# Low parts of the weights on GpSimd in block 0, and all kernel blocks of the convolution made in block 0

## The chip, the cores and the metric

The kernel runs on one core of one Trainium2 chip. Its time is the device time of one execution in microseconds; of the kernel before there are three runs, and their median is the time that counts. A profile is one further execution, recorded by the hardware, with a time of its own.

## The reference, cut to what is computed

A layer in two halves on `x` of shape 1 x 2048 x 576, all in float32: a state-space convolution along the sequence, and a feed-forward part of width 4608.

```
mod = (silu(c) @ w_mod).reshape(1, 6, 1, 576)          # sa, ca, ga, sb, cb, gb
h = layernorm(x) * (1 + ca) + sa
P = exp((A * dt)[:, :, None] * arange(2048))           # 576 x 128 x 2048, complex
K = 2 * einsum("dn,dnl->dl", C * dt, P).real           # one kernel of 2048 taps per channel
x = x + ga * (causal_convolution(h, K) + h * D_skip)   # by FFT of length 4096
h = layernorm(x) * (1 + cb) + sb
x = x + gb * (relu(h @ w1) @ w2)                       # w1 576 x 4608, w2 4608 x 576
```

## The kernel before, in words

**Four blocks of the sequence.** The 2048 positions are cut into 4 blocks of 512 (`NB`). For each block there is a convolution, `conv(s)` for s = 0 to 3, and then a feed-forward part over 36 tiles of 128 hidden units (`NF`). The feed-forward part of all four blocks is one loop of 144 tiles in `ffn` (L1401). `conv(0)` and everything that leads to it run ahead of that loop. `conv(1)`, `conv(2)` and `conv(3)` run inside it, one block ahead: `conv(1)` beside tiles 0 to 35, and so on. What runs beside the tiles of a block is a Python generator: `block0`, `block1`, `block2` (L774 to L793).

**The tiles.** float32 precision comes from three products: a weight `r` is rounded to a high part `w` by ScalarE (`hi1`, `hi2`), and the low part is what is left, `r - w` (`lo1`, `lo2`). In block 0 the low parts are computed, three subtractions a tile: 128x640 (L1296), 128x64 (L1307) and 128x512 (L1308). They are also stored to device memory, and blocks 1 to 3 load them from there. `first(g)` makes 14 matmuls of 128x512 into `hps`. ScalarE then makes the high part `hh` of the activation, and VectorE the low part `hl` (L1332). `second(g)` makes 14 more matmuls into the five accumulators `acc`, one tile later. Two buffers hold the raw `r1`, three the raw `r2`, and three each the split `w1` and `w2`; a raw buffer is free when its low part has been computed.

**The convolution kernels.** The 2048 taps fall into four kernel blocks of 512. Kernel block 0 is made ahead of the loop. Kernel blocks 1 to 3 are made by `rest` from tables `W1d`, `Zd`, `W2d` in device memory, for twelve groups of 48 channels (`NH`). For a group, `rots` turns a table of 128 x 2 x 48 x 16 by a complex factor, once for every kernel block. One such turn, `rot`, is four VectorE instructions: two products of 128x1536 (L481, L483) and two sums of 128x768 (L485, L487). Then `products` makes 192 small matmuls into `kps`, in two halves that ScalarE empties into `ke`. The tables come in by DMAs from GpSimd's queue in written order (`load0`, `load2`), ahead of use, into 3 buffers for `W0` and `Z` and 2 for `W2`.

In the kernel before, `block0` makes kernel blocks 1 to 3 of groups 0 to 5 and kernel block 1 alone of groups 6 to 11: 24 turns. `conv(1)` needs no more than that. `block1` loads the tables of groups 6 to 11 once more and makes their kernel blocks 2 and 3: 12 turns.

**What sets the order.** `step(g)` is called four times in a tile and takes work from the block's generator (L1362). The generator yields estimated VectorE microseconds, or `None` for work of TensorE. `rate` gives the work per step that is aimed at; `room` limits what may be taken within any four steps. What a block's generator has not yielded by its last tile is drained there (L1428). In the program that results, a scheduler of the framework decides each engine's order, except for instructions marked as kept in program order. Every engine then runs its own queue in order, and waits at an instruction whose inputs or buffers aren't ready.

Of the kernel before, what the change touches and what calls it, by code (L numbers as in the profile page):

```python
# [10 lines left out]
F32 = mybir.dt.float32  # L11
# [7 lines left out]
P = 128  # L19
# [5 lines left out]
NF = F // P  # L25
G = 96
NG = 6
H = 48
# [21 lines left out]
class KGen:  # L50
# [400 lines left out]
                out=self.k.kd[s][p][64 * t : 64 * t + 64], in_=ke[t::2]  # L451
            )

    def rest(self, psum, plan):

        nc, k = self.nc, self.k
        v = nc.vector.tensor_tensor
        hs = list(plan)
        with ExitStack() as ctx:
            pt = k.pool(ctx, f"kr{len(hs)}", side="right")  # L460
            d = Kept(k.tc, nc.gpsimd).dma_start

            def load0(h):
# [23 lines left out]
                v(out[:, 1], out[:, 1], T[:, 0], op=ALU.add)  # L487
                yield 0.95

            def rots(h, W1, W0, Z):  # L490
                blocks = plan[h]
                a = [W1[:, :, :, 16 * i : 16 * i + 16] for i in range(len(blocks))]
                if blocks[0] == 1:
                    yield from rot(a[0], W0, Z, 0)
                    if len(blocks) > 1:
                        yield from rot(a[1], W0, Z, 1)
                        yield from rot(a[2], a[0], Z, 1)
                else:
                    yield from rot(a[0], W0, Z, 1)
                    yield from rot(a[1], a[0], Z, 0)  # L500

            ke = {}

            def products(h, W1, W2):
                blocks = plan[h]
                na = 16 * len(blocks)
                if h % 6 == 0:
                    ke[h // 6] = pt.tile([P, na, 72], F32, tag=f"ke{na}", bufs=1, name=f"ker_{h}")
                for half in range(2):
                    ps = psum.tile([P, 6, na], F32, tag="cps", bufs=1, name="kps")  # L510
                    for q in range(6):
                        for dd in range(4):
                            ch = dd * 12 + 6 * half + q
                            for r in range(2):
                                nc.tensor.matmul(  # L515
                                    ps[32 * dd : 32 * dd + 32, q, :],
                                    W2[:, r, ch],
                                    W1[:, r, ch],
                                    start=(r == 0),
                                    stop=(r == 1),  # L520
                                )
# [3 lines left out]
                    nc.scalar.activation(  # L525
                        ke[h // 6][:, :, q0 : q0 + 6], ps.rearrange("p q a -> p a q"), AF.Copy
                    )
                    yield None
                if h % 6 == 5:
                    yield -1  # L530
                    for i, s in enumerate(blocks):
# [5 lines left out]
            nxt = [load0(hs[0])]  # L537
            W2 = load2(hs[0])
            nxt.append(load0(hs[1]))
            for _ in range(1 if len(hs) == NH else 7):  # L540
                yield -1
            prev = iter(())
            for i, h in enumerate(hs):
                W0, Z = nxt.pop(0)
                if i + 2 < len(hs):
                    nxt.append(load0(hs[i + 2]))
                na = 16 * len(plan[h])
                bufs = 1 if len(plan[h]) != len(plan[hs[i - 1]]) else 2
                W1 = pt.tile([P, 2, H, na], F32, tag=f"W1{na}", bufs=bufs, name=f"W1r_{h}")
                yield from spread(rots(h, W1, W0, Z), prev, len(plan[h]))  # L550
                prev = products(h, W1, W2)
                if i + 1 < len(hs):
                    W2 = load2(hs[i + 1])
            yield from prev


# [9 lines left out]
class Body:  # L566
# [195 lines left out]
    def main(self, ctx, kg, hooks):  # L762
# [496 lines left out]
    def ffn(self, gens):  # L1259
# [102 lines left out]
        def step(g):  # L1362
# [194 lines left out]
```

## Time and profile before

| what | value |
|---|---|
| median of 3 runs | 1340.26 us (1336.31 to 1343.84) |
| the profiled execution: its time, its span | 1346.28 us, 1344.5 us |
| mean granted TensorE clock | 0.934 |
| first low part `hl` of the activation: tile 0, 36, 72, 108 | 233.6, 570.0, 847.0, 1105.0 us |
| last `hl` (tile 143) | 1328.1 us |
| VectorE, whole span | 895.8 us busy, 1324 instructions |
| GpSimd, whole span | 162.5 us busy, 260 instructions |

The work ahead of the loop takes the first 227 us or so. After it the blocks can be told apart in the trace by the first `hl` of each: block 0 runs to about 562 us, block 1 to about 846, block 2 to about 1106, block 3 to the end. How to read it: in a span of four stages with different limits, the shares over the whole span say little, and each block is looked at by itself. A busy TensorE is not the same as a TensorE at its peak, since the granted clock changes.

### The profile page before, as it was taken

What the parts mean: (1) busy time and instruction counts of PE and PEld (TensorE: products, weight loads), DVE (VectorE), ACT (ScalarE), POOL (GpSimd) and SP (SyncE); (2) the same over time, 40 slices, a digit from 0 to 9 for tenths busy, and PEclk for the clock granted to TensorE, in tenths of its full rate; (3) what the DMA queues carried; (4) which work ended last, traced back from release to release, by engine and by line L of the source; (5) the groups of instructions that cost most, each with busy time, mean ns of one, the idle gap of its engine ahead of it and who ended that gap; (6) DMA issues with size and microseconds to landing.
All of it is one profiled execution on the core that took longest, in us unless ns stands there. A gap on an engine that the chain in (4) does not pass through costs nothing.

```text
span 1344.5 us, 26011 instructions
## 1 busy us (share of the span) xinstructions
PE 1218.3 (91%) x10720; PEld 963.8 (72%) x10720; DVE 895.8 (67%) x1324; ACT 494.6 (37%) x863; POOL 162.5 (12%) x260
## 2 busy tenths in 40 slices
PE   4565686889989998999999999999999999999997
PEld 3344564667768676777777887887888888888885
DVE  5999978997995999768658995467996221111112
ACT  5688523222223422622234225433323352323331
POOL 0656501001100100011001000100000000000000
PEclk9556767999999998999999999999999999999998
DMA  8567972987878877698889995867996667666661
GB/s 269 218 231 291 307 272 80 346 298 273 320 279 288 297 247 290 206 400 322 281 276 339 346 357 160 275 219 271 349 392 189 176 178 230 193 197 199 199 177 53
DMA packets 122379, 345.85 MB, mean 257 GB/s; under 512 B 23916, under 2 KB 24212, under 8 KB 111508
## 3 DMA queue, kind: packets, MB, share of 16 engines
q1 hardware_dynamic: 105364, 226.96, 50.9%
q0 software_dynamic: 16384, 115.85, 23.0%
q8 instruction: 84, 1.38, 0.4%
q10 hardware_dynamic: 512, 1.38, 0.3%
q14 instruction: 35, 0.29, 0.1%
HBM read 262.73 MB, written 81.40 MB: 256 GB/s over the span
## 4 chain that ended last, share of the span: by engine, by line
PE 72%; DVE 14%; DMA 7%; issue 4%; ACT 2%; POOL 1%; ACTq 0%; POOLq 0%; DVEq 0%; SPq 0%
PE acc L1352 29%; PE hps L1326 28%; DMA r<-in_w_dram 4%; PE ps_f L846 4%; PE kps L71 2%; PE ph L71 2%; PE kps L515 2%; PE ps_i L1053 2%; DVE W1r L483 2%; DVE T L481 2%; DMA L2d<-w 1%; DVE W1r L487 1%; DVE W1r L485 1%; DVE T L62 1%; DVE w L1296 1%
## 5 line engine op out<-in xcount | busy, mean ns | idle before, releaser
L1326 PE MATMUL hps<-xh,w 128*128 128x512 f32 x1152 | 393.6, 402 | 1.9 <-issue 1.1
L1352 PE MATMUL acc<-w,hh 128*128 128x512 f32 x1152 | 370.6, 403 | 12.9 <-ACT hh L1331 12.9
L1332 DVE SCALAR_TENSOR_TENSOR hl<-hps,hh 128x512 fp32r<-128x512 f32 x144 | 99.1, 688 | 310.1 <-ACT hh L1331 309.3
L1352 PEld LDWEIGHTS acc<-w,hh 128*128 128x128 f32 x1152 | 216.3, 189 | 60.7 <-ACT hh L1331 14.5
L1326 PEld LDWEIGHTS hps<-xh,w 128*128 128x128 f32 x1152 | 218.5, 190 | 50.2 <-issue 1.6
L1326 PE MATMUL hps<-xl,w 128*128 128x512 f32 x576 | 229.7, 400 | 0.1
L1352 PE MATMUL acc<-w,hl 128*128 128x512 f32 x576 | 223.0, 399 | 0.9 <-DVE hl L1332 0.9
L1331 ACT ACTIVATE hh<-hps 128x512 fp32r<-128x512 f32 x144 | 85.8, 596 | 289.7 <-PE hps L1326 289.4
L1301 ACT ACTIVATE w<-r 128x576 fp32r<-128x576 f32 x141 | 96.7, 686 | 231.0 <-PE acc L1352 219.5
L1291 ACT ACTIVATE w<-r 128x640 fp32r<-128x640 f32 x140 | 102.7, 733 | 92.8 <-DMA r<-in_w_dram 92.8
L1326 PEld LDWEIGHTS hps<-xl,w 128*128 128x128 f32 x576 | 109.3, 190 | 23.9 <-DVE xl L47 0.6
L1352 PEld LDWEIGHTS acc<-w,hl 128*128 128x128 f32 x576 | 107.9, 189 | 24.7 <-DVE hl L1332 2.1
L1326 PE MATMUL hps<-xs,w 128*128 128x512 f32 x288 | 98.6, 413 | 0.0
L71 PE MATMUL kps<-W,W 128*32 128x16 f32 x2304 | 39.9, 211 | 45.3 <-POOL W L68 28.1
L1032 DVE TENSOR_TENSOR Y<-Y,T 128x1152 f32<-128x1152 f32 x60 | 79.4, 1351 | 0.0
L71 PEld LDWEIGHTS kps<-W,W 128*32 128x32 f32 x2304 | 35.1, 144 | 59.0 <-POOL W L68 30.8
L847 ACT ACTIVATE Z<-ps_f 128x288 f32<-128x288 f32 x120 | 48.8, 408 | 70.2 <-PE ps_f L846 68.8
L515 PEld LDWEIGHTS kps<-W1r,W2r 128*32 128x32 f32 x3456 | 44.7, 113 | 37.7 <-issue 19.0
L515 PE MATMUL kps<-W1r,W2r 128*32 128x48 f32 (+2 forms) x3456 | 52.1, 201 | 14.6 <-ACT ker L525 9.3
L1471 POOL DMA_DIRECT2D out_dram<-x x16 | 8.7, 544 | 468.6 <-DVE x L1463 466.3
L1326 PEld LDWEIGHTS hps<-xs,w 128*128 128x128 f32 x288 | 54.0, 191 | 11.3
L1352 PE MATMUL acc<-hl,w 128*128 128x512 f32 x144 | 56.7, 394 | 0.0
(235 smaller groups left out, 1586.6 us busy)
## 6 DMA issues: line engine op xcount, KB each, us to landing
r<-in_w_dram SPq DMA_DIRECT2D x144, 320.0 KB, 7.3
r<-in_w_dram SPq DMA_DIRECT2D x144, 288.0 KB, 5.1
w<-L1d SPq DMA_DIRECT2D x108, 320.0 KB, 3.2
w<-L2d SPq DMA_DIRECT2D x108, 288.0 KB, 2.8
W2r<-W2d POOLq DMA_DIRECT2D x18, 1536.0 KB, 9.2
W2d<-W SPq DMA_DIRECT2D x12, 1536.0 KB, 8.6
Ua<-Ud POOLq DMA_DIRECT2D x15, 1152.0 KB, 9.6
W<-W1d POOLq DMA_DIRECT2D x18, 768.0 KB, 10.6
```

The lines of the kernel that those rows point to most:

```text
L71: self.tc.keep_in_program_order(self.nc.tensor.matmul(*args, **kw))
L481: v(T, X, zi, op=ALU.mult)
L515: nc.tensor.matmul(ps[32 * dd : 32 * dd + 32, q, :], W2[:, r, ch], W1[:, r, ch], start=(r == 0), stop=(r == 1),)
L846: nc.tensor.matmul(o, fc[:, n2, c, :], src(n2), start=True, stop=True)
L847: ev = nc.scalar.activation(Z[:, n2, c], ps[:, :PC], AF.Copy)
L1032: v(y, y, T, op=op or ALU.add)
L1291: copy(g - 1)(w1[g][:, 0], r1[g], AF.Copy)
L1301: copy(g)(w[:, 0:D], r2[g], AF.Copy)
L1326: nc.tensor.matmul(ps, a, x, start=(i == 0), stop=(i == 13))
L1331: nc.scalar.activation(hh, ps, AF.Relu)
L1332: nc.vector.scalar_tensor_tensor(hl, ps, 0.0, hh, op0=ALU.max, op1=ALU.subtract)
L1352: nc.tensor.matmul(acc[i], a, x, start=(f == 0 and seen[i] == 1), stop=(f == NF - 1 and seen[i] == (3 if i < 4 else 2)),)
```

## The change

Three things are changed together.

1. `vec(g)`, the engine that subtracts for the low parts, becomes GpSimd for tiles 3 to 35. For tiles 0 to 2 it stays VectorE. The results and the stores are the same.
2. `rest` makes kernel blocks 1 to 3 of all twelve groups in one pass, in `block0`, in the order 0 to 11: 36 turns. The call in `block1` is gone, and with it the second loads of six groups' tables and the six groups' second pass of small matmuls. The small matmuls of groups 6 to 11 in block 0 are 48 columns wide and not 16.
3. The numbers that set the pace: `room` in block 0 goes from 7.5 to 10.2, `rate` from 2.15 to 2.5 in block 0 and from 1.8 to 1.27 in block 1.

```diff
-    def rest(self, psum, plan):
+    def rest(self, psum):
...
-            def rots(h, W1, W0, Z):
-                blocks = plan[h]
-                a = [W1[:, :, :, 16 * i : 16 * i + 16] for i in range(len(blocks))]
-                if blocks[0] == 1:
-                    yield from rot(a[0], W0, Z, 0)
-                    if len(blocks) > 1:
-                        yield from rot(a[1], W0, Z, 1)
-                        yield from rot(a[2], a[0], Z, 1)
-                else:
-                    yield from rot(a[0], W0, Z, 1)
-                    yield from rot(a[1], a[0], Z, 0)
+            def rots(W1, W0, Z):
+                a = [W1[:, :, :, 16 * i : 16 * i + 16] for i in range(3)]
+                yield from rot(a[0], W0, Z, 0)
+                yield from rot(a[1], W0, Z, 1)
+                yield from rot(a[2], a[0], Z, 1)
...
-            for _ in range(1 if len(hs) == NH else 7):
-                yield -1
+            yield -1
...
         def block0():
             self.x2p.append(self.pool(ctx, "x2b"))
-            yield from kg.rest(
-                self.cps, {h: (1, 2, 3) if h < 6 else (1,) for h in (0, 6, 1, 7, 2, 8, 3, 9, 4, 10, 5, 11)}
-            )
+            yield from kg.rest(self.cps)
...
             yield -1
             self.cvs.close()
-            yield from kg.rest(self.cps, {h: (2, 3) for h in range(6, NH)})
             pool(2)
             yield from self.conv(2)
...
         def vec(g):
-            return (Kept(self.tc, nc.vector) if g < 3 else nc.vector).tensor_tensor
+            return (Kept(self.tc, nc.vector) if g < 3 else nc.gpsimd).tensor_tensor
...
-            room = (7.5, 7.0, 7.0, 7.0)[g // NF] - sum(recent[-3:])
+            room = (10.2, 7.0, 7.0, 7.0)[g // NF] - sum(recent[-3:])
...
-        return (2.15, 1.8, 1.4, 0.5)[b]
+        return (2.5, 1.27, 1.4, 0.5)[b]
```

In the changed kernel the line numbers behind the first of these edits are smaller by up to 14: L1282, L1293, L1294 there are L1296, L1307, L1308 here, L1318 is L1332, and L1016 and L1018 are L1030 and L1032.

**GpSimd's queue in block 0.** Before it holds only DMA issues there. `W2r`, `W` and `Zr` are the tables of one group, each read from its place in device memory.

```order
L47 DMA W2r_3074<-W2d_71 128x3072
L47 DMA W_7_3076<-W1d_84 128x1536
L47 DMA Zr_3077<-Zd_96 128x192
L47 DMA W2r_3233<-W2d_66 128x3072
L47 DMA W_2_3235<-W1d_79 128x1536
L47 DMA Zr_3236<-Zd_91 128x192
```

In the changed kernel the same place, from the load of the fourth group's `W2r` on, reads as follows. `w` is a split weight and `r` its raw form; the two low parts of 64 and 512 columns belong to tiles 5 and 6, those of 640 columns to tiles 7 and 8.

```order
L47 DMA W2r_3268<-W2d_67 128x3072
L47 DMA W_4_3270<-W1d_81 128x1536
L1293 TENSOR_TENSOR w_3339<-r_3071,w_3339 128x64
L1294 TENSOR_TENSOR w_3339<-r_3071,w_3339 128x512
L1293 TENSOR_TENSOR w_3442<-r_3176,w_3442 128x64
L1294 TENSOR_TENSOR w_3442<-r_3176,w_3442 128x512
L1282 TENSOR_TENSOR w_3345<-r_3286,w_3345 128x640
L47 DMA Zr_3271<-Zd_93 128x192
L1282 TENSOR_TENSOR w_3448<-r_3416,w_3448 128x640
L47 DMA W2r_3475<-W2d_68 128x3072
```

The subtractions of two tiles now stand between the loads of one group and those of the next, behind DMAs that wait for a buffer.

**VectorE in block 0, between one `hl` and the next but one.** Before, the turns of the tables (`T`, `W1r`) stand among the subtractions for the low parts (`w<-r,w`).

```order
L1332 SCALAR_TENSOR_TENSOR hl<-hps,hh 128x512
L485 TENSOR_TENSOR W1r_2993<-W1r_2993,T 128x48x16
L487 TENSOR_TENSOR W1r_2993<-W1r_2993,T 128x48x16
L1307 TENSOR_TENSOR w_3094<-r_2942,w_3094 128x64
L481 TENSOR_TENSOR T<-W_6_2967,Zr_2968 128x1536
L1308 TENSOR_TENSOR w_3094<-r_2942,w_3094 128x512
L1296 TENSOR_TENSOR w_3033<-r_3001,w_3033 128x640
L483 TENSOR_TENSOR W1r_3080<-W_6_2967,Zr_2968 128x1536
L483 TENSOR_TENSOR W1r_3239<-W_1_2989,Zr_2990 128x96x16
L485 TENSOR_TENSOR W1r_3080<-W1r_3080,T 128x768
L487 TENSOR_TENSOR W1r_3080<-W1r_3080,T 128x768
L1332 SCALAR_TENSOR_TENSOR hl<-hps,hh 128x512
```

In the changed kernel there are only turns between them.

```order
L1318 SCALAR_TENSOR_TENSOR hl<-hps,hh 128x512
L485 TENSOR_TENSOR W1r_3274<-W1r_3274,T 128x48x16
L487 TENSOR_TENSOR W1r_3274<-W1r_3274,T 128x48x16
L483 TENSOR_TENSOR W1r_3481<-W_3_3062,Zr_3063 128x96x16
L481 TENSOR_TENSOR T<-W_2_2989,Zr_2990 128x1536
L483 TENSOR_TENSOR W1r_3274<-W1r_3274,Zr_2990 128x96x16
L485 TENSOR_TENSOR W1r_3274<-W1r_3274,T 128x48x16
L487 TENSOR_TENSOR W1r_3274<-W1r_3274,T 128x48x16
L483 TENSOR_TENSOR W1r_3481<-W_3_3062,Zr_3063 128x96x16
L481 TENSOR_TENSOR T<-W1r_3274,Zr_2990 128x1536
L1318 SCALAR_TENSOR_TENSOR hl<-hps,hh 128x512
```

The three turns of a group take the place of one turn and the subtractions. A group's turns are spread over two tiles, so that the twelve groups end with tile 23; before, the 24 turns end with tile 18.

**VectorE behind the last `hl` of block 0 (tile 35).** Before, the convolution of the next block is done there but for its last rounding (`xs`, `xl`) and the output of the block before (`oT`, `x_0`).

```order
L1332 SCALAR_TENSOR_TENSOR hl<-hps,hh 128x512
L1157 TENSOR_TENSOR xs_6168<-xf,xs_6168 64x512
L1159 TENSOR_TENSOR xl_6167<-xf,xh_6166 128x512
L1467 TENSOR_TENSOR oT<-oT,m_gb 128x512
L1159 TENSOR_TENSOR xl_6167<-xf,xh_6166 128x512
L1469 TENSOR_TENSOR x_0_281<-x_0_281,oT 128x512
```

In the changed kernel, half of the second spectral product (`Y`) and the whole butterfly behind it (`W`, `V`) stand there first.

```order
L1318 SCALAR_TENSOR_TENSOR hl<-hps,hh 128x512
L1016 TENSOR_TENSOR T<-Ka,Ua 128x1152 x2
L1018 TENSOR_TENSOR Y_1_6154<-Y_1_6154,T 128x4x288 x2
L1016 TENSOR_TENSOR T<-Ka,Ua 128x1152 x2
L1018 TENSOR_TENSOR Y_1_6154<-Y_1_6154,T 128x4x288 x2
L846 TENSOR_TENSOR W<-Y_1_6154 128x576
L847 TENSOR_TENSOR W<-Y_1_6154 128x576
L846 TENSOR_TENSOR W<-Y_1_6154 128x576
L847 TENSOR_TENSOR W<-Y_1_6154 128x576
L853 TENSOR_TENSOR V_1_6265<-W 128x576
```

The tail of `conv(1)` has moved from ahead of the last tiles of block 0 to behind them.

More of the change, by code (lines that the diff above doesn't have):

```diff
@@ L452, in store @@
             )
-    def rest(self, psum, plan):
+    def rest(self, psum):
         nc, k = self.nc, self.k
         v = nc.vector.tensor_tensor
-        hs = list(plan)
+        na = 48
         with ExitStack() as ctx:
-            pt = k.pool(ctx, f"kr{len(hs)}", side="right")
+            pt = k.pool(ctx, "kr", side="right")
             d = Kept(k.tc, nc.gpsimd).dma_start
@@ L488, in rot @@
                 yield 0.95
[L490 to L500 removed]
+            def rots(W1, W0, Z):
[3 more added lines that the diff above has]
+                yield from rot(a[2], a[0], Z, 1)
             ke = {}
             def products(h, W1, W2):
[L505 to L506 removed]
                 if h % 6 == 0:
[L508 removed]
+                    ke[h // 6] = pt.tile([P, na, 72], F32, tag="ke", bufs=1, name=f"ker_{h}")
                 for half in range(2):
@@ L530, in products @@
                     yield -1
-                    for i, s in enumerate(blocks):
+                    for i, s in enumerate((1, 2, 3)):
                         self.store(
@@ L535, in products @@
                         )
-            nxt = [load0(hs[0])]
-            W2 = load2(hs[0])
-            nxt.append(load0(hs[1]))
-            for _ in range(1 if len(hs) == NH else 7):
-                yield -1
+            nxt = [load0(0)]
+            W2 = load2(0)
+            nxt.append(load0(1))
+            yield -1
             prev = iter(())
-            for i, h in enumerate(hs):
+            for h in range(NH):
                 W0, Z = nxt.pop(0)
[L545 to L550, printed above, removed]
+                if h + 2 < NH:
+                    nxt.append(load0(h + 2))
+                W1 = pt.tile([P, 2, H, na], F32, tag="W1", bufs=2, name=f"W1r_{h}")
+                yield from spread(rots(W1, W0, Z), prev, 3)
                 prev = products(h, W1, W2)
-                if i + 1 < len(hs):
-                    W2 = load2(hs[i + 1])
+                if h + 1 < NH:
+                    W2 = load2(h + 1)
             yield from prev
```

## The prediction

> **What bounds the kernel now.** I read the page's totals and slices first, then one window for each stage, then the instruction groups of block 0, then the waits.
>
> ```profile
> PE 1218.3 (91%) x10720; PEld 963.8 (72%) x10720; DVE 895.8 (67%) x1324; ACT 494.6 (37%) x863; POOL 162.5 (12%) x260
> DVE  5999978997995999768658995467996221111112
> POOL 0656501001100100011001000100000000000000
> 560.75 0.59 ACT L1436 ACTIVATE o<-acc 128x512 f32<-128x512 f32 x1
> 846.91 0.59 ACT L1436 ACTIVATE o<-acc 128x512 f32<-128x512 f32 x1
> 1104.87 0.59 ACT L1436 ACTIVATE o<-acc 128x512 f32<-128x512 f32 x1
> ```
>
> The slices show VectorE (DVE) full early and idle late, and GpSimd (POOL) almost idle from slice 8 on. The rows of L1436 are the evacuations that end blocks 0, 1 and 2. With them the loop is cut into windows:
>
> ```profile
> core 0: us, PE busy (x) PEld busy (x) DVE busy (x) ACT busy (x) POOL busy (x), PEclk, DMA share, GB/s
> 227.00:410.00 183.00, 162.41 (x2621) 124.99 (x2622) 164.69 (x176) 46.45 (x85) 18.50 (x35) 0.93 0.78 283
> 410.00:562.00 152.00, 146.57 (x796) 113.13 (x794) 127.88 (x218) 56.30 (x110) 9.29 (x15) 0.98 0.80 284
> 562.00:846.00 284.00, 280.09 (x2298) 222.55 (x2298) 210.02 (x267) 101.87 (x188) 24.83 (x43) 1.00 0.84 302
> 846.00:1106.00 260.00, 260.00 (x1143) 210.97 (x1142) 165.96 (x232) 96.94 (x175) 12.35 (x22) 1.00 0.76 258
> 1106.00:1331.00 225.00, 225.00 (x998) 186.46 (x997) 29.78 (x45) 66.44 (x106) 2.17 (x4) 1.00 0.62 184
> ```
>
> Blocks 2 and 3 are TensorE's (PE): busy all the time at clock 1.00, 260 us with a convolution beside the tiles and 225 without. Block 1 is nearly so. Block 0, 335 us in two rows, is different. While the tables are turned, VectorE is busy for 165 of 183 us, and TensorE has gaps and a clock of 0.93. Block 0 would take TensorE about as long as block 2 with the small matmuls added, some 295 us. So **VectorE sets the pace of block 0, TensorE that of block 1**, and the change moves work from the second to the first.
>
> **The change part by part.**
>
> Block 1 first. Its second pass of the small matmuls goes, and 12 turns.
>
> ```profile
> L515 PE MATMUL kps<-W1r,W2r 128*32 128x32 f32 x1152 | 16.5, 200 | 3.9 <-ACT ker L525 3.9
> L515 PE MATMUL kps<-W1r,W2r 128*32 128x48 f32 (+2 forms) x3456 | 52.1, 201 | 14.6 <-ACT ker L525 9.3
> ```
>
> What is left is a convolution beside 36 tiles, as in block 2: 284 - 260 = 24 us. The matmuls and their waits account for 16.5 + 3.9 = 20.4 of it. I take **-22**, with 20 and 24 as ends. The six groups of 48 instead of 16 columns in block 0 cost next to nothing: the whole of L515 is 52.1 us for three equal counts, of which the 32-column third took 16.5.
>
> Now VectorE in block 0 (groups between 227 and 562 us).
>
> ```profile
> L481 DVE TENSOR_TENSOR T<-W,Zr 128x1536 f32<-128x1536 f32 x18 | 31.5, 1748 | 0.0
> L483 DVE TENSOR_TENSOR W1r<-W,Zr 128x1536 f32<-128x1536 f32 x18 | 31.3, 1750 | 9.6 <-PE kps L515 9.6
> L1296 DVE TENSOR_TENSOR w<-r,w 128x640 fp32r<-128x640 f32 x33 | 26.9, 816 | 1.4 <-ACT w L1291 1.4
> L1332 DVE SCALAR_TENSOR_TENSOR hl<-hps,hh 128x512 fp32r<-128x512 f32 x36 | 24.6, 683 | 16.0 <-ACT hh L1331 16.0
> L487 DVE TENSOR_TENSOR W1r<-W1r,T 128x768 f32<-128x768 f32 x24 | 22.8, 948 | 0.0
> L485 DVE TENSOR_TENSOR W1r<-W1r,T 128x768 f32<-128x768 f32 x24 | 22.7, 947 | 0.0
> L1308 DVE TENSOR_TENSOR w<-r,w 128x512 fp32r<-128x512 f32 x33 | 22.5, 681 | 0.0
> L1307 DVE TENSOR_TENSOR w<-r,w 128x64 fp32r<-128x64 f32 x33 | 7.1, 216 | 4.7 <-ACT w L1301 4.7
> ```
>
> Removed are the subtractions of tiles 3 to 35: 26.9 + 22.5 + 7.1 = 56.5 us. A turn is two products and two sums, 1.75 + 1.75 + 0.95 + 0.95 = 5.4 us; twelve more are 64.8. The balance is **+8**. So far the parts nearly cancel, and the kernel would gain the 22 us of block 1 less this.
>
> But the subtractions don't vanish; they run on GpSimd, beside a VectorE that is almost always busy. The trace has one place where both engines work on operands that lie in SBUF, and two to compare it with:
>
> ```profile
> 132.65 3.91 POOL L68 TENSOR_TENSOR W<-T,T 128x384 f32<-128x384 f32 x4 [5.88 <-DVE T L62]
> 132.49 1.81 DVE L62 TENSOR_TENSOR T<-W,Zp 128x768 f32<-128x768 f32 x2
> 155.44 4.93 POOL L68 TENSOR_TENSOR W<-T,T 128x384 f32<-128x384 f32 x4 [8.41 <-DVE T L62]
> 157.00 4.65 DVE L47 TENSOR_TENSOR W<-Z 128x576 f32<-128x576 f32 x4
> 157.37 1.52 POOL L68 TENSOR_TENSOR W<-T,T 128x384 f32<-128x384 f32 x1
> 157.94 1.56 DVE L47 TENSOR_TENSOR W<-Z 128x576 f32<-128x576 f32 x1
> 164.39 2.75 DVE L47 TENSOR_TENSOR W<-Z 128x576 f32<-128x576 f32 x4
> 144.83 1.15 POOL L68 TENSOR_TENSOR zs<-zs,E 128x192 f32<-128x192 f32 x2
> ```
>
> Four GpSimd sums take 3.91 us beside VectorE products that read one operand from PSUM (`Zp`), and those aren't slowed. Beside butterflies with both operands in SBUF (`W<-Z`), the same four take 4.93, and four butterflies 4.65 instead of 2.75. The single rows show why: each 0.98 us sum and each 0.69 us butterfly is stretched to about 1.5, with starts 0.57 apart. They take turns. VectorE loses 1.52 - 0.69 = 0.8 us to a sum of 0.98, or 0.82 of it.
>
> [...]
>
> Turns, butterflies and spectral products all read two SBUF operands; `hl` reads one from PSUM. So nearly every subtraction moved will hold up VectorE. How long is one? From the rows above, 384 columns take 3.91 / 4 = 0.98 us, 192 take 1.15 / 2 = 0.575, so 2.1 ns a column: 1.52 us for 640, 1.25 for 512, 0.31 for 64, together 3.08 a tile as an estimate, against 1.71 on VectorE. For 33 tiles that is 102 us of GpSimd. VectorE can be held up only where it isn't idle (292.6 of 335 us busy) nor at `hl` (24.6 us): 268 of 335, or 0.80. The loss is 102 x 0.82 x 0.80 = **+67**. Its ends are 0, if the two run side by side, and 102, if all is lost.
>
> [...]
>
> The last part is the order at the end of block 0. Behind the last `hl` stand eight instructions of 128x1152 and a butterfly that now end before tile 35. From rows of the trace these are 17 us:
>
> ```profile
> L1032 DVE TENSOR_TENSOR Y<-Y,T 128x1152 f32<-128x1152 f32 x12 | 15.9, 1351 | 0.0
> 535.61 0.75 DVE L860 TENSOR_TENSOR W<-Y 128x576 f32<-128x576 f32 x1
> 540.73 0.45 DVE L874 TENSOR_TENSOR V<-W 128x288 f32<-128x288 f32 x1
> ```
>
> That is 8 x 1.35 + 6 x 0.75 + 4 x 0.45, counting the whole butterfly. TensorE has one `second` left, 14 matmuls, to cover it. The work itself is in VectorE's sum already, but less of the chain behind it lies under tiles. Between 0 and 17 I take **+8**.
>
> The waits in the queues:
>
> ```profile
> POOL W2r L47 <- PE kps L515: 99.7, 10, 16.1
> ACT w L1291 <- DMA r<-in_w_dram: 82.6, 19, 11.2
> PE acc L1352 <- DVE hl L1332: 0.9, 2, 0.7
> L47 POOL DMA_DIRECT2D W2r<-W2d x18 | 9.5, 528 | 157.7 <-PE kps L515 150.8 <-DVE xl L47 6.1 <-DMA out_dram<-x 0.8
> ```
>
> GpSimd waits for TensorE up to 16.1 us at the load of `W2r`, which hurts nobody today. In the changed kernel five subtractions stand behind it, and tiles 5 to 7 wait for them. Released, the queue needs two DMA issues of 0.53, five subtractions (4.64) and, between them, a VectorE product of 1.7 each: some 14 us, while TensorE has about half that to do. It stalls, but VectorE has a group of turns, 16.2 us, to do meanwhile and remains what is waited for; I take 0. ScalarE's waits for raw weights, 82.6 us, could fall, because buffers no longer wait for VectorE's queue, or rise, if GpSimd is late; 0 as well. New pace numbers only decide where the sum above falls.
>
> The sum against the profiled execution: 1346.3 - 22 + 8 + 67 + 8 = 1407. That execution lies 6 us above the median of the runs, 1340.3; so **1401**, and I say 1400.
>
> **The rivals.**
>
> *The engines run side by side.* Block 0 grows by 8 + 8, block 1 falls by 22, and the median becomes 1334; without the tail 1326. This would be faster by up to 1%. For it speaks that only a handful of instructions in the trace show the turn-taking. Against it, every pair that meets there does. It decides at VectorE: if a tile's subtractions cost it under 6 / 33 = 0.18 us of their 3.08, the change gains.
>
> *GpSimd's queue becomes the bound.* If the 14 us behind each `W2r` add to two tiles of TensorE (2 x 225 / 36 = 12.5 us, from block 3) rather than lie beside the turns, a group takes 27 us instead of 16.2 of turns, 1.3 of `hl` and some 5 of lost turns. Twelve times 4.5 is 54 more: 1455. Tiles queue up two deep, which speaks against it.
>
> *Half the collisions.* If subtractions fall mostly into VectorE's gaps, as a loss of 33 would mean, the time is 1367, in the range of the forecast. If only a fifth of 67 is left, it is 1347, no change to speak of.
>
> **How the numbers follow.** Forecast and half collisions together 0.78, side by side 0.10, hardly any loss 0.05, queue-bound 0.07. The forecast's lower end is some 1350 (a quarter of the loss and no tail), the upper 1440 (all 102 us lost: 1346 - 20 + 8 + 102 + 8 - 6 = 1438). As range I give 1345 to 1440. A measurement of this kernel can tell about 0.5% from no change, 7 us. Side by side is mostly faster: 0.08 faster, 0.07 the same, 0.85 slower.
>
> **What would show it.** Right: turns of L481 and L483 in block 0 above 2.5 us in the mean, GpSimd's 128x640 subtraction stretched beyond 1.6 us, block 0 above 390 us, block 1 near 260, blocks 2 and 3 as before. Wrong: turns that stay at 1.75 us. If block 0 is long but turns are not, look for TensorE waiting for `w` from GpSimd; that would be the queue. If block 1 stays above 275 us, the 22 us were not the small matmuls'.

## The result, and the profile after

The changed kernel takes 1421.03 us (median of 4 runs, 1415.44 to 1422.81), the kernel before 1342.05 in 4 runs on the same chip (1336.31 to 1345.79). The ratio is 1.0585, 95% interval 1.0536 to 1.0635: slower, and 21 us above the forecast of 1400, inside its range. The profiled execution after took 1421.08 us with a span of 1418.9, so 74.4 us more span than before (1344.5). One of the four executions of run 2 below took 1450.7 us at a granted clock of 0.812, against 0.933 to 0.939 in its other three, and its median is of those three.

First the page of the changed kernel: totals, and busy tenths by slice.

```profile
PE 1225.5 (86%) x9568; PEld 970.7 (68%) x9568; DVE 917.4 (65%) x1225; ACT 495.1 (35%) x851; POOL 325.1 (23%) x341
...
DVE  5889968999999949874549852264999232110102
...
POOL 0667311746556444301001000010100000000000
PEclk9556678889999899867999999999999999999999
```

VectorE has 99 instructions fewer than before (1225 against 1324) and is yet busy for 21.6 us more. GpSimd, almost idle before from slice 8 on, works in slices 8 to 17, which lie in block 0. The clock dips at slices 18 and 19, at the end of that block.

To compare stages I cut both kernels at the same events: the first `hl`, the end of the last turn, the `hl` of tile 35, that of tile 36 (the first of block 1), and of tiles 72 and 108. The rows are, in this order, the turns, the rest of block 0 up to its last tile ("convolution"), the tail between two `hl`, block 1 and block 2. Before:

```profile
core 0: us, PE busy (x) PEld busy (x) DVE busy (x) ACT busy (x) POOL busy (x), PEclk, DMA share, GB/s
233.60:403.70 170.10, 149.92 (x2463) 115.44 (x2463) 157.98 (x166) 40.73 (x74) 17.59 (x34) 0.94 0.83 302
403.70:556.40 152.70, 147.27 (x922) 113.75 (x914) 127.84 (x218) 52.91 (x105) 9.29 (x15) 0.97 0.77 273
556.40:570.00 13.60, 13.60 (x72) 10.91 (x71) 8.85 (x15) 11.43 (x21) 0.49 (x1) 1.00 0.63 203
570.00:847.00 277.00, 273.09 (x2260) 216.77 (x2259) 202.66 (x254) 95.90 (x178) 24.34 (x43) 1.00 0.85 306
847.00:1105.00 258.00, 258.00 (x1134) 209.32 (x1133) 165.26 (x231) 95.36 (x173) 12.35 (x22) 1.00 0.76 259
```

After:

```profile
234.80:497.20 262.40, 206.63 (x2779) 163.79 (x2777) 257.94 (x178) 56.94 (x97) 152.19 (x104) 0.90 0.69 241
497.20:616.30 119.10, 102.01 (x573) 76.58 (x574) 90.33 (x114) 34.50 (x71) 46.36 (x43) 0.90 0.76 267
616.30:661.20 44.90, 28.05 (x94) 18.25 (x93) 31.97 (x59) 17.48 (x32) 0.19 (x1) 0.66 0.15 45
661.20:921.50 260.30, 255.86 (x1106) 206.08 (x1105) 139.80 (x206) 92.45 (x166) 15.08 (x25) 0.99 0.78 264
921.50:1179.50 258.00, 258.00 (x1134) 209.37 (x1133) 165.20 (x231) 95.31 (x172) 12.35 (x22) 1.00 0.76 259
```

Block 0 is 426.4 us instead of 336.4 (+90.0), block 1 260.3 instead of 277.0 (-16.7), block 2 is the same. All of the growth of block 0 lies in the turns: +92.3, with VectorE busy for 258 of 262 us while TensorE idles for 56. Convolution and tail together are 164.0 against 166.3: what the tail gained, the stretch ahead of it lost.

VectorE's groups in the turns of the changed kernel (busy us, mean ns of one, idle time before them):

```profile
L487 DVE TENSOR_TENSOR W1r<-W1r,T 128x768 f32<-128x768 f32 x36 | 53.0, 1474 | 0.0
L483 DVE TENSOR_TENSOR W1r<-W,Zr 128x1536 f32<-128x1536 f32 x24 | 52.2, 2178 | 4.2 <-PE kps L507 4.2
L481 DVE TENSOR_TENSOR T<-W,Zr 128x1536 f32<-128x1536 f32 x24 | 47.4, 1974 | 0.1
L485 DVE TENSOR_TENSOR W1r<-W1r,T 128x768 f32<-128x768 f32 x36 | 46.0, 1277 | 0.1
L481 DVE TENSOR_TENSOR T<-W1r,Zr 128x1536 f32<-128x1536 f32 x12 | 28.3, 2360 | 0.0
L483 DVE TENSOR_TENSOR W1r<-W1r,Zr 128x1536 f32<-128x1536 f32 x12 | 23.4, 1952 | 0.0
L1318 DVE SCALAR_TENSOR_TENSOR hl<-hps,hh 128x512 fp32r<-128x512 f32 x23 | 15.6, 679 | 1.2 <-ACT hh L1317 1.2
```

The code of a turn is unchanged, but its two products and two sums take 6.96 us in the mean (2.10 + 2.10 + 1.28 + 1.47) where they took 5.39, while `hl`, which reads one operand from PSUM, is as short as before (679 ns against 683). The timeline shows how (start, us, engine, line):

```profile
402.11 0.95 DVE L487 TENSOR_TENSOR W1r<-W1r,T 128x768 f32<-128x768 f32 x1
...
402.98 1.75 DVE L483 TENSOR_TENSOR W1r<-W,Zr 128x1536 f32<-128x1536 f32 x1
...
403.15 1.76 POOL L1293 TENSOR_TENSOR w<-r,w 128x64 fp32r<-128x64 f32 x1 [2.67 <-ACT w L1287]
...
404.64 1.88 DVE L481 TENSOR_TENSOR T<-W1r,Zr 128x1536 f32<-128x1536 f32 x1
...
404.87 2.80 POOL L1294 TENSOR_TENSOR w<-r,w 128x512 fp32r<-128x512 f32 x1
...
406.44 2.84 DVE L483 TENSOR_TENSOR W1r<-W,Zr 128x1536 f32<-128x1536 f32 x1
...
407.63 3.04 POOL L1282 TENSOR_TENSOR w<-r,w 128x640 fp32r<-128x640 f32 x1
...
409.21 2.28 DVE L485 TENSOR_TENSOR W1r<-W1r,T 128x768 f32<-128x768 f32 x1
```

The 64-column subtraction, 0.31 us at its shortest, has a record of 1.76 us and ends at 404.91, just behind the product of L483 (404.73). The next one, 1.27 us at its shortest, ends at 407.67, 1.2 us behind the product of L481 (406.52). The product that started meanwhile ends at 409.28, 1.6 us later, and takes 2.84 us instead of 1.75. Each engine's record holds the other's share: they take turns.

I add up, over VectorE's instructions in block 0, what each takes beyond the short ones of its operation and shape (the tenth percentile). This **stretch** is 73.1 us after. Some 57 of it lie in the turns and 16 behind them.

### The profile page after: what moved, and what is told of

The parts are those of the page before. It is cut to its first block, busy times and chain, and to the rows that moved or that the text cites. A ratio compares the mean times of both kernels' runs of the same rounds, so it can differ in the third digit from the quotient of the medians.

```text
span 1418.9 us, 23668 instructions
## 1 busy us (share of the span) xinstructions
PE 1225.5 (86%) x9568; PEld 970.7 (68%) x9568; DVE 917.4 (65%) x1225; ACT 495.1 (35%) x851; POOL 325.1 (23%) x341
## 3 DMA queue, kind: packets, MB, share of 16 engines
q0 software_dynamic: 14368, 101.10, 18.8%
## 4 chain that ended last, share of the span: by engine, by line
PE 60%; DVE 28%; DMA 6%; issue 4%; ACT 2%; POOL 1%; POOLq 0%; ACTq 0%; DVEq 0%
PE acc L1338 24%; PE hps L1312 24%; DVE T L481 5%; DVE W1r L483 4%; PE ps_f L832 4%; DVE W1r L487 3%; DVE W1r L485 3%; DMA Ua<-Ud 3%; DVE T L1016 2%; PE ps_i L1039 2%; PE kps L71 2%; PE ph L71 2%; DVE Y L1018 1%; DMA kt<-kd 1%; PE kps L507 1%
## 5 line engine op out<-in xcount | busy, mean ns | idle before, releaser
L1338 PE MATMUL acc<-w,hh 128*128 128x512 f32 x1152 | 362.0, 399 | 0.6 <-DMA w<-L2d 0.6
L1318 DVE SCALAR_TENSOR_TENSOR hl<-hps,hh 128x512 fp32r<-128x512 f32 x144 | 99.0, 688 | 370.6 <-ACT hh L1317 370.1
L1338 PE MATMUL acc<-w,hl 128*128 128x512 f32 x576 | 232.4, 416 | 26.9 <-DVE hl L1318 26.9
L1312 PE MATMUL hps<-xl,w 128*128 128x512 f32 x576 | 226.4, 393 | 0.1
L1338 PEld LDWEIGHTS acc<-w,hl 128*128 128x128 f32 x576 | 111.5, 196 | 53.9 <-DVE hl L1318 30.4
L1277 ACT ACTIVATE w<-r 128x640 fp32r<-128x640 f32 x140 | 102.6, 733 | 29.3 <-DMA r<-in_w_dram 29.2
L507 PE MATMUL kps<-W1r,W2r 128*32 128x48 f32 x2304 | 46.1, 246 | 41.7 <-issue 22.3
L1018 DVE TENSOR_TENSOR Y<-Y,T 128x1152 f32<-128x1152 f32 x60 | 80.8, 1378 | 0.0
L507 PEld LDWEIGHTS kps<-W1r,W2r 128*32 128x32 f32 x2304 | 40.8, 135 | 56.1 <-issue 30.3
L1282 POOL TENSOR_TENSOR w<-r,w 128x640 fp32r<-128x640 f32 x33 | 74.2, 2252 | 15.3 <-ACT w L1277 11.7
L1294 POOL TENSOR_TENSOR w<-r,w 128x512 fp32r<-128x512 f32 x33 | 65.5, 1983 | 0.0
```

The source lines that it names most:

```text
L507: nc.tensor.matmul(ps[32 * dd : 32 * dd + 32, q, :], W2[:, r, ch], W1[:, r, ch], start=(r == 0), stop=(r == 1),)
L1018: v(y, y, T, op=op or ALU.add)
L1277: copy(g - 1)(w1[g][:, 0], r1[g], AF.Copy)
L1282: vec(g)(w[:, 1], r, w[:, 0], op=ALU.subtract)
L1294: v(w[:, 640:], r[:, :512], w[:, :512], op=ALU.subtract)
L1312: nc.tensor.matmul(ps, a, x, start=(i == 0), stop=(i == 13))
```

## The experiments

In the expectations A is the turn-taking, B the two engines side by side, C GpSimd's queue as the bound; D is the place at which the pace numbers put the work. All ratios are to the kernel before, run on the same chip. Times in us, stages as above, from the profiled execution of each kernel. There is one profile of each: the first `hl`, though the work ahead of it is much the same, comes between 228.9 and 234.8 us in the fourteen, so a few us in a stage say little.

| kernel | median | turns | convolution + tail | block 1 | stretch |
|---|---|---|---|---|---|
| before | 1342.05 | 170.1 | 152.7 + 13.6 | 277.0 | 2.0 |
| after | 1421.03 | 262.4 | 119.1 + 44.9 | 260.3 | 73.1 |
| 1: low parts on VectorE | 1371.43 | 226.9 | 134.4 + 23.0 | 260.4 | 3.0 |
| 2: GpSimd, old plan | 1370.10 | 176.7 | 176.4 + 6.3 | 280.8 | 59.4 |
| 3: ScalarE copies | 1352.12 | 208.1 | 109.5 + 46.2 | 258.7 | 2.0 |
| 4: GpSimd memsets | 1350.76 | 208.4 | 102.6 + 48.9 | 258.4 | 1.9 |
| 5: pace numbers up | 1407.88 | 254.3 | 141.2 + 22.4 | 259.7 | 72.0 |
| 6: GpSimd copies | 1370.76 | 224.3 | 110.6 + 43.8 | 260.1 | 22.8 |
| 7: half the low parts | 1397.86 | 235.5 | 139.5 + 33.7 | 259.5 | 33.6 |
| 8: turns later | 1390.88 | 125.0 | 194.1 + 6.3 | 349.1 | 2.0 |
| 9: one buffer of `hps` | 1410.5 | 252.1 | 146.2 + 22.5 | 258.2 | 68.2 |
| 10: 9, factor in PSUM | 1372.52 | 225.4 | 138.5 + 22.8 | 258.7 | 30.8 |
| 11: 2, factor in PSUM | 1370.15 | 173.3 | 170.3 + 6.4 | 287.2 | 36.6 |
| 12: 3, pace numbers up | 1349.78 | 207.7 | 123.7 + 33.7 | 260.8 | 1.5 |

**1. The turns alone.** The changed kernel, with the subtractions back on VectorE.

```diff
-            return (Kept(self.tc, nc.vector) if g < 3 else nc.gpsimd).tensor_tensor
+            return (Kept(self.tc, nc.vector) if g < 3 else nc.vector).tensor_tensor
```

> The changed kernel with the low parts of tiles 3 to 35 back on VectorE; all twelve groups stay in block 0. Theory A (GpSimd's subtractions and VectorE's instructions with two SBUF operands exclude each other): VectorE no longer loses the 68 us by which its instructions in block 0 are stretched, and gets 56.5 us of subtractions, so the time is 1421 - 68 + 57 = 1410 us, 1395 to 1422; turns take 1.75 us again. Theory B (the engines run side by side, block 0 grew by its turns and its tail alone): 1421 + 57 = 1478 us. Theory C (what costs is the wait of TensorE for low parts stuck in GpSimd's queue): 1360 to 1390 us.

It takes 1371.43 us, 1.0235 (1.0201 to 1.0269). That is faster than A's number and in C's. The windows of turns, convolution and tail:

```profile
230.70:457.60 226.90, 193.12 (x2719) 147.09 (x2718) 226.89 (x230) 52.12 (x89) 18.44 (x34) 0.91 0.72 256
457.60:592.00 134.40, 120.53 (x654) 90.07 (x653) 114.94 (x182) 40.13 (x79) 8.12 (x14) 0.94 0.78 274
592.00:615.00 23.00, 18.57 (x75) 13.52 (x74) 14.06 (x37) 16.44 (x31) 0.18 (x1) 0.78 0.27 89
```

VectorE is busy all through the turns. Twelve more turns, with the new pace numbers, lengthen this stage by 56.8 us against before, and convolution and tail shrink by 8.9. Turns are 5.38 us again. So the subtractions on GpSimd cost 50 us against the same subtractions on VectorE (1421 - 1371). Why the rest differs from A's number, run 3 shows.

**2. The low parts alone.** The kernel before, with only its subtractions on GpSimd (24 turns in block 0 as before).

```diff
-            return (Kept(self.tc, nc.vector) if g < 3 else nc.vector).tensor_tensor
+            return (Kept(self.tc, nc.vector) if g < 3 else nc.gpsimd).tensor_tensor
```

> The kernel before with one line changed: the low parts of tiles 3 to 35 on GpSimd; turns stay split over blocks 0 and 1, pace numbers as before. Theory A: VectorE gives up 56.5 us and loses some 60, so 1342 + 4 us, 1335 to 1360. Theory B: VectorE is relieved of 56.5 us where it sets the pace, 1290 to 1310 us. Theory C: the queue holds up TensorE here too, above 1365 us.

1370.10 us, 1.0226 (1.0189 to 1.0264). B is ruled out: relieving VectorE of 56.5 us makes this kernel slower, a turn takes 6.91 us and the stretch is 59.4. The time is above A's range too, and in C's. The turns stage is 6.6 us longer than before, so the stretch about eats the relief there; 23.7 us come in the convolution:

```profile
405.60:582.00 176.40, 156.82 (x823) 121.01 (x822) 128.21 (x171) 60.33 (x117) 83.02 (x67) 0.94 0.74 249
```

VectorE's busy time there is that of before (128.2 against 127.8), TensorE has 19.6 us of idle instead of 5.4 and a lower clock, and GpSimd's waits in this window are these (us in total, times, longest):

```profile
POOL w L1307 <- ACT w L1301: 42.1, 10, 11.1
...
POOL w L1307 <- DMA kd<-ker: 9.2, 1, 9.2
...
POOL w L1296 <- DMA L2d<-w: 6.8, 1, 6.8
```

The subtractions stand in order behind waits of the queue. But TensorE's own waits in this window are others, and they add up to its idle time: 6.7 us for `hl`, 5.6 for `V`, 4.6 for the DMA of `kt` and 2.6 for `x`. None is for a low part, so it is not shown that the queue holds TensorE up here. The other 9.5 of the 23.7 us are TensorE busy for longer (156.8 against 147.3) at a clock of 0.94 instead of 0.97. Why `hl`, `V` and `x` come late stays open.

**3. No subtraction on either engine.** ScalarE writes the low parts as copies of the raw weights; the low parts are not computed.

```diff
-            return (Kept(self.tc, nc.vector) if g < 3 else nc.gpsimd).tensor_tensor
+            if g < 3:
+                return Kept(self.tc, nc.vector).tensor_tensor
+            return lambda out, r, hi, op: nc.scalar.activation(out, r, AF.Copy)
```

> The changed kernel with the three subtractions of tiles 3 to 35 replaced by ScalarE copies of the raw weights, so the low parts are not computed and neither VectorE nor GpSimd does anything for them. Theory A: the 68 us of stretching go and nothing comes in their place: 1350 us, 1335 to 1365, with turns at 1.75 us. Theory B: VectorE's work is unchanged, 1410 to 1425 us. Theory C: 1350 to 1380 us, but then turns were not what got shorter.

1352.12 us, 1.0091 (1.0061 to 1.0121), as A said. The three windows:

```profile
229.40:437.50 208.10, 193.27 (x2778) 153.49 (x2777) 201.61 (x178) 87.54 (x168) 18.42 (x34) 0.98 0.84 303
437.50:546.90 109.40, 99.95 (x573) 75.62 (x574) 75.53 (x113) 45.98 (x99) 8.13 (x14) 0.94 0.83 288
546.90:593.10 46.20, 28.65 (x94) 18.94 (x93) 31.95 (x58) 17.49 (x32) 0.16 (x1) 0.67 0.15 53
```

Against the changed kernel, with the same order of turns, VectorE's busy time in the turns is 56.3 us less (257.9 to 201.6) and the stage 54.3 us shorter. Against run 1 it tells what the relief is worth: the turns are 18.8 us shorter for 25.3 us less of VectorE's work, convolution and tail together 1.7 us shorter for 21.5 less. In the convolution TensorE is busy for 100 of 109 us, and a VectorE with less to do gains next to nothing.

**4. GpSimd at work, without reading.** Memsets of the same tiles in place of the subtractions; the low parts are zero.

```diff
+            return lambda out, r, hi, op: nc.gpsimd.memset(out.bitcast(F32), 0.0)
```

> The changed kernel with the three subtractions of tiles 3 to 35 replaced by GpSimd memsets of the same tiles: the low parts are zeros. They stand in GpSimd's queue as the subtractions did, write as much and read nothing. Theory A with reads as what excludes: turns at 1.75 us and 1350 us, 1335 to 1370, as with the copies on ScalarE. Theory A with any GpSimd instruction excluding: turns stretched by as much as the memsets last. Theory C: low parts still stand behind waiting loads in the queue, so most of the loss stays, above 1390 us.

1350.76 us, 1.0075 (1.0037 to 1.0112), no different from run 3 by the intervals. A group of GpSimd and one of VectorE during the turns:

```profile
L1273 POOL MEMSET w<- 128x640 f32 x26 | 16.6, 638 | 32.6 <-PE hps L1314 26.5 <-DMA L1d<-w 6.0
```

```profile
L481 DVE TENSOR_TENSOR T<-W,Zr 128x1536 f32<-128x1536 f32 x24 | 41.9, 1748 | 0.1
```

GpSimd works beside the turns, and they stay at 1748 ns. Here work on GpSimd that only writes costs VectorE nothing; what costs is the reading. (A memset doesn't wait for the raw weights, so it stands at other moments than a subtraction.)

**5. The pace.** The changed kernel with higher numbers for block 0, so that VectorE's other work is issued earlier.

```diff
-            room = (10.2, 7.0, 7.0, 7.0)[g // NF] - sum(recent[-3:])
+            room = (14.0, 7.0, 7.0, 7.0)[g // NF] - sum(recent[-3:])
-        return (2.5, 1.27, 1.4, 0.5)[b]
+        return (3.2, 1.27, 1.4, 0.5)[b]
```

> The changed kernel with only its pace numbers for block 0 raised: room 14.0 for 10.2, rate 3.2 for 2.5. In the changed kernel 44.9 us pass between the last hl of block 0 and the first of block 1, against 13.6 before. Theory A alone (the sum of VectorE's work and of what it is held up by sets block 0, whatever the order): 1421 us, 1412 to 1430. Theory D (the tail is a cost of its own that comes from where the generator's work is placed): the stretch of 44.9 us shrinks below 30 and the time falls by 10 to 25 us, 1396 to 1411.

1407.88 us, 1.0489 (1.0443 to 1.0536): 13 less than after, with the tail 22.5 shorter and the convolution 22.1 longer. The time and the shorter tail are as D said, and the time is below A's range. But convolution and tail together are the same (163.6 against 164.0), so D's mechanism isn't what gained: the tail is work that has moved. The gain is in the turns (8.1 us) and ahead of the first `hl`, which comes 5.7 us earlier.

**6. GpSimd reading once.** A copy of the raw weights in place of the subtraction; the low parts are not computed.

```diff
+            return lambda out, r, hi, op: nc.gpsimd.tensor_copy(out, r)
```

> The changed kernel with the three subtractions of tiles 3 to 35 replaced by GpSimd copies of the raw weights: one SBUF operand is read instead of two, and the low parts are not computed. Theory A with any read of SBUF by GpSimd excluding: a turn above 5.7 us in the mean and a time between the 1351 us of the memsets and 1421 us, 1360 to 1395. Theory A with only a second operand excluding: turns at 5.4 us and 1346 to 1357 us.

1370.76 us, 1.0215 (1.0172 to 1.0258). During the turns:

```profile
L1273 POOL CAST w<-r 128x640 fp32r<-128x640 f32 x26 | 41.3, 1600 | 6.5 <-issue 5.9 <-POOL w L1273 0.4
```

A copy of 640 columns takes 713 ns at its shortest and 1600 here; turns are 5.86 us and the stretch is 22.8. One read is enough to be in VectorE's way, and less work there makes for less stretch.

**7. Half the low parts.** For tiles 3 to 35 the 128x640 subtraction goes back to VectorE, the other two stay.

```diff
-                vec(g)(w[:, 1], r, w[:, 0], op=ALU.subtract)
+                (nc.vector.tensor_tensor if g > 2 else vec(g))(w[:, 1], r, w[:, 0], op=ALU.subtract)
```

> The changed kernel with one of the three subtractions, the one of 128x640, back on VectorE and the two of 64 and 512 columns on GpSimd. Theory A: the stretch falls in proportion to GpSimd's time beside VectorE, from 73 us in block 0 to some 40, and 24 us of subtractions come back to VectorE; between the two ends measured (1371 and 1421 us) 1396, 1385 to 1407. Theory C (lateness in GpSimd's queue): with half the work in the queue most of the lateness goes, below 1385 us.

1397.86 us, 1.0407 (1.0362 to 1.0453), with a stretch of 33.6, as A said. Half of GpSimd's subtracting leaves half the loss: 26 of the 50 us above run 1.

**8. Turns moved the other way.** The kernel before with block 1 of the kernel alone in block 0 (12 turns), blocks 2 and 3 of all groups in block 1.

```diff
-                self.cps, {h: (1, 2, 3) if h < 6 else (1,) for h in (0, 6, 1, 7, 2, 8, 3, 9, 4, 10, 5, 11)}
+                self.cps, {h: (1,) for h in range(NH)}
...
-            yield from kg.rest(self.cps, {h: (2, 3) for h in range(6, NH)})
+            yield from kg.rest(self.cps, {h: (2, 3) for h in range(NH)})
...
-            room = (7.5, 7.0, 7.0, 7.0)[g // NF] - sum(recent[-3:])
+            room = (7.5, 9.5, 7.0, 7.0)[g // NF] - sum(recent[-3:])
...
-        return (2.15, 1.8, 1.4, 0.5)[b]
+        return (1.75, 2.3, 1.4, 0.5)[b]
```

> A version in the other direction, from the kernel before: block 0 makes kernel block 1 of all groups (12 turns), block 1 makes kernel blocks 2 and 3 of all groups (24 turns); low parts on VectorE; rate 1.75 and 2.3 and room 9.5 in block 1. If block 0 is VectorE's and block 1 TensorE's: block 0 falls by some 28 us to 308, TensorE's own work; block 1 gets 12 turns and six more passes of small matmuls, 16 to 28 us more. Sum 1330 to 1342 us against 1342. If VectorE then bounds block 1 too (210 + 65 us busy of some 300): 1345 to 1360.

1390.88 us, 1.0366 (1.0317 to 1.0416): a miss of both ranges. Block 0 falls by 10.9 us and not 28, block 1 grows by 72.1. Block 0 behind its turns, block 1 up to its last evacuation, and from there to the first `hl` of block 2:

```profile
356.70:550.90 194.20, 191.86 (x1135) 151.39 (x1134) 144.54 (x247) 72.03 (x136) 8.13 (x14) 0.98 0.75 257
557.20:888.60 331.40, 308.24 (x3406) 237.30 (x3405) 264.67 (x301) 93.74 (x178) 34.35 (x61) 0.95 0.84 304
888.60:906.30 17.70, 14.58 (x61) 10.54 (x61) 9.99 (x21) 13.80 (x26) 0.16 (x1) 0.81 0.23 66
```

In block 0 the turns are 45.1 us shorter and the convolution 41.4 longer, with TensorE busy for 191.9 of 194.2 us: it is the bound there, and fewer turns gain little. In block 1 TensorE is busy for 308 of 331 us, at a clock of 0.95 instead of 1.00, VectorE for 265, and a tail of 17.7 us has come up. I did not follow block 1 further.

**9 and 10. The disputed read.** Run 9 is the changed kernel with one buffer of `hps` instead of two, which frees room in PSUM. Run 10 uses the room: ScalarE copies the turn's factor `Z` there, so that the products of L481 and L483 read only one operand from SBUF. The sums of L485 and L487 still read two, and GpSimd's subtractions are the same.

```diff
-            ps = self.fps.tile([P, 512], F32, tag="hps", bufs=2, name="hps")
+            ps = self.fps.tile([P, 512], F32, tag="hps", bufs=1, name="hps")
```

> Control for the next run: the changed kernel with one buffer instead of two for hps, which frees one bank of PSUM. Nothing else. TensorE's next first(g) then waits for hl of the tile before, which second(g) waits for one step later anyway: 1421 to 1445 us.

```diff
+        self.zp = self.pool(ctx, "zps", space=PSUM).tile([P, 2, 2, 2, H], F32, name="zp")
...
-                W0, Z = nxt.pop(0)
+                W0, Zs = nxt.pop(0)
+                Z = k.zp[:, h % 2]
+                nc.scalar.activation(Z, Zs, AF.Copy)
```

> The control, with the complex factor of the turns copied by ScalarE into the freed PSUM bank, so that the two products of a turn (L481, L483) read one operand from SBUF and one from PSUM; the two sums (L485, L487) read two from SBUF as before. GpSimd's subtractions are unchanged. Theory A with two SBUF operands as the condition: the products return to 1.75 us, the sums and the instructions of conv(1) are still stretched, so less than half of the 73 us remains, and the time falls by 30 to 50 us under the control. If any VectorE instruction beside a GpSimd subtraction were slowed, or theory C: products above 2 us and the control's time within 10 us.

Run 9: 1410.5 us, 1.0505 (1.0474 to 1.0536), 11 less than after instead of none or more; the order came out otherwise, with a tail of 22.5. Run 10: 1372.52 us, 1.0218 (1.0191 to 1.0245), 38 less than run 9. Two of VectorE's groups during the turns, in run 9:

```profile
L483 DVE TENSOR_TENSOR W1r<-W,Zr 128x1536 f32<-128x1536 f32 x24 | 55.2, 2303 | 0.0
...
L487 DVE TENSOR_TENSOR W1r<-W1r,T 128x768 f32<-128x768 f32 x36 | 44.9, 1246 | 0.0
```

In run 10:

```profile
L487 DVE TENSOR_TENSOR W1r<-W1r,T 128x768 f32<-128x768 f32 x36 | 43.1, 1198 | 0.0
...
L483 DVE TENSOR_TENSOR W1r<-W,zp 128x1536 f32<-128x1536 f32 x24 | 41.9, 1747 | 0.0
```

The product is back at 1747 ns (all four groups of products are at 1747 to 1750) with every subtraction still beside it; the sum, with two operands from SBUF, is still stretched (945 to 950 ns undisturbed). The stretch is 37.4 us less than in run 9, and the time 38. This tells the turn-taking from the queue: GpSimd has the same instructions in both.

**11. The old plan with the factor in PSUM.** Run 2 with the edits of runs 9 and 10.

> The kernel before with the low parts of tiles 3 to 35 on GpSimd (as in e2_gpsimd_old_plan), one hps buffer, and the factor of the turns in PSUM. Theory A: of the 59 us of stretching in e2 some 25 remain, while VectorE is relieved of 48 us of subtractions: 1371 - 30 = 1340 us, 1325 to 1350; below 1342 if a single hps buffer costs nothing. Theory C: as e2, 1360 us or more.

1370.15 us, 1.0188 (1.0156 to 1.022): a miss for A, in C's range. Against run 2 the stretch falls from 59.4 to 36.6 and block 0 from 359.4 to 350.0, but block 1 grows from 280.8 to 287.2. The convolution stays long (170.3). TensorE is idle for 16.6 us of it, and its waits put 14.0 of these to `hps`, whose single buffer `hl` must free first; run 2, with two buffers, has no wait at `hps` there. TensorE waits for no low part. So the single buffer, which run 11 has and run 2 hasn't, costs something here; why `hl` comes late when GpSimd makes the low parts of the old plan stays open.

**12. The pace without subtractions.** Run 3 with the pace numbers of run 5.

> The kernel of e3_lows_scalar (ScalarE copies of the raw weights in place of the subtractions; low parts not computed) with the raised pace numbers of e5_pace_up. e1_lows_vector differed from e3 in two ways at once: 48 us of subtractions on VectorE, and a tail of 23.0 us against 46.2. If both hold block 0 up, each by its own amount, the tail here falls below 30 us and the time by 8 to 15 us, to 1337 to 1344, so that the subtractions on VectorE are worth some 30 us at an equal tail. If the tail is only where VectorE's remaining work happens to lie, the time stays at 1352, within 5 us.

1349.78 us, 1.0065 (1.0041 to 1.0088), 2 less than run 3, with the tail 12.5 shorter and the convolution 14.2 longer. So the tail was not a cost of its own. None of the twelve is faster than the kernel before.

## Why the prediction was right, and where its sum was not

*GpSimd's reads hold up VectorE: +67 forecast, 63 to 67 measured.* Block 0 is 62.6 us longer after than in run 3, and 66.5 longer than in run 4; the medians differ by 69 and 70. Runs 4, 6 and 10 show the mechanism from three sides: no stretch without GpSimd's read (1.9 us in run 4, products of a turn at 1747 to 1750 ns), less of it where GpSimd reads one operand instead of two (22.8 us in run 6 against 73.1), and none in the instructions of VectorE that take one operand from PSUM (products at 1747 to 1750 ns in run 10, `hl` at 679 ns in the changed kernel). The forecast of 0.66 of GpSimd's undisturbed time (0.82 lost at a meeting, times 0.80 for how often they meet) also held in size: the shortest subtractions are 1.54, 1.27 and 0.31 us, 3.12 a tile and 103 us for 33, and the stretch of 73.1 is 0.71 of that. No run tells the two factors apart. The loss in time is less than the stretch: in the turns, where VectorE is the bound, VectorE is busy for 56.3 us more than in run 3 and the stage is 54.3 longer; behind them it is busy for 14.8 more, and convolution and tail are 8.3 longer. How much of these 8.3 is the lower clock there (0.90 against 0.94 in the convolution) is not told apart.

Of the signs named beforehand, block 0 (426 us), block 1 (260) and the 128x640 subtraction (2.25 us in the mean) came as said. One did not: the products of L481 and L483 were to be above 2.5 us and are 2.10. The sums share the stretch: they take 1.28 and 1.47 us where they took 0.95.

*Balance of VectorE: +8 forecast, and wrong in its make-up.* The forecast let 64.8 us of turns and 56.5 of subtractions pass one to one into the time. Twelve turns and the new pace numbers cost block 0 47.9 us (run 1 against before), and taking the subtractions off VectorE gives back 20.5 (run 3 against run 1): +27.4 with the tail in it, where the forecast had 8 + 8. The one term was 17 us too large and the other 36; that they have opposite signs and, with the tail's 8, leave an error of only 11 is luck. The step that failed is "VectorE sets the pace of block 0". It does so while the tables are turned. In the stage behind them TensorE was busy for 147 of 153 us before, and the 21.5 us of VectorE's work taken away there gave 1.7. The row of 410 to 562 us in the prediction shows that TensorE was busy for 146.6 of 152.0; it was read for the block and not for its second half. A smaller part is that the durations of instructions in a row overlap: L487 and L483 in the timeline above start 0.87 us apart (402.11 and 402.98) where a sum of 0.95 stands between, and the subtractions' 56.5 us are 46.8 in VectorE's busy time of block 0 (355.9 in run 1, 309.1 in run 3).

*The tail: +8 forecast, at most 17; the interval grew by 31.3.* It was mis-sized: VectorE has 32.0 us of work between the two `hl`, 8.9 before, and TensorE waits for it. The instructions that the forecast counted do end 17.3 us behind the `hl` of tile 35, at 633.6; but the inverse transform and the layer norm that hang on them, which ran beside the last tiles before, and the rounding behind those now take from there to 661.2. The longest wait of TensorE there:

```profile
PE ps_i L1039 <- DVE V L853: 9.6, 1, 9.6
```

But it is no loss by itself: the convolution ahead is 33.6 us shorter, and runs 5 and 12 move 22 and 12 us of tail back with little change to convolution and tail together (163.6 against 164.0, 157.4 against 155.7).

*Block 1: -22 forecast, -16.7 measured.* TensorE's busy time fell by 17.2 us (273.1 to 255.9), about the 16.5 of the matmuls; its idle time did not fall (3.9 before, 4.4 after). The forecast's window began at 562, just behind the last evacuation of block 0 (560.75), and the first `hl` of block 1 comes only at 570.0: it took in the end of `conv(1)`. By the first `hl` blocks 1 and 2 take 277 and 258 us, 19 apart and not 24.

*The queues: 0 forecast.* TensorE's waits during block 0 of the changed kernel:

```profile
PE acc L1338 <- DVE hl L1318: 26.9, 8, 11.1
PE kps L507 <- issue: 22.3, 10, 4.3
PE kps L507 <- DVE W1r L487: 11.6, 11, 1.9
```

The first and the third are for VectorE's work. The second is put to nothing ("issue"), but each of its ten waits ends 0.1 to 0.5 us behind a sum of a turn (L485, L487), which points to VectorE again. TensorE has no wait there for a `w` of GpSimd, VectorE has 4.5 us of idle time in the turns, and GpSimd's longest wait at `W2r` is 7.9 us where it was 16.1. So the rival of the queue, which had 1455, isn't what happened here. Side by side (1326 to 1334) is ruled out by runs 2, 4 and 10.

*The range.* Its lower end was to be a quarter of the loss and no tail. By the prediction's own terms that is 1340 - 22 + 8 + 17 = 1343 and not "some 1350"; nothing hangs on it, as the time came out in the upper half.

The sum, by the spans: turns and pace +47.9, subtractions off VectorE -20.5, turn-taking +62.6, block 1 -16.7, together +73.3 of 74.4. The forecast's sum was +61. Its largest term held, 4 us too high; balance and tail together were 11 us too low, and 5 us too much was taken off for block 1. So the 13 us by which the sum is off are much smaller than the errors inside its balance.

## What to carry to other kernels

Before elementwise work moves from a full VectorE to an idle GpSimd, look where both read their operands: here each us of GpSimd's subtractions took 0.7 us from VectorE instructions with two operands in SBUF, together more than the subtractions had cost on VectorE (73 against 56.5 us). One operand put into PSUM (run 10), or a form on GpSimd that only writes (run 4), took the products out of the conflict: their groups are at 1747 to 1750 ns in the mean in both runs, where the changed kernel has 1952 to 2360. And relief counted in the stage where VectorE was the bound (18.8 us for 25.3 in the turns) and hardly behind it (1.7 for 21.5), so cut the windows by stage before adding up busy times.

## What was unexpected of the hardware

How sharply it follows the read was not expected: memsets on GpSimd leave a turn at 5.39 us, copies with one read make it 5.86, subtractions with two 6.96. In proportion to the work, too: the copies' shortest times, 0.71, 0.24 and 0.61 us, make 51 us for 33 tiles, of which 22.8 came back as stretch (0.44), against 0.71 for the subtractions. Why a copy takes less was not tried.
